# A state-space layer beside attention: chunked states and a scan replaced by a direct causal convolution

## The chip, the cores and the metric

The kernel runs on one core of a Trainium2 chip. A core has five engines, each with its own instruction stream in a fixed order: TensorE (PE) multiplies matrices, VectorE (DVE) and ScalarE (ACT) work on elements, GpSimd (POOL) and SyncE (SP) here mostly issue DMAs. The engines wait for one another by semaphores. The metric is the time of one execution on the device, in microseconds (us); the median of two executions before the change is 853.1 us (852.64 and 853.55).

## The reference

`x` has 2048 positions and 512 channels, all tensors are bf16. Two layers run on their inputs, and a gate mixes their outputs:

```python
g = sigmoid((x * gate_w).sum(-1, keepdims=True))
a = attention(x, wqkv, wo)          # 32 heads of 16, softmax over 2048 keys, not causal
dt = exp(log_dt)[:, None]           # B: 512 channels, 128 states each, complex
logdA = dt * (A_re + 1j * A_im);  dB = dt * (B_re + 1j * B_im);  C = C_re + 1j * C_im
P = exp(logdA[:, :, None] * arange(2048))
K = einsum("dn,dnl,dn->dl", C, P, dB).real      # 2048 taps for each channel
y = causal_convolution(u, K) + u * Dskip        # by an FFT in the reference
out = g * a + (1 - g) * y
```

The tap `K[d, l]` is a sum over 128 states of a coefficient times a complex root to the power `l`. The kernel reads `x` as the input of both layers.

## The kernel before, in words

**Attention.** The 2048 x 2048 scores of 32 heads are cut into 32 batches of four heads by 512 queries, and each batch into 64 tiles of 128 keys by 512 queries: 2048 tiles. Three tiles form a group (683 groups, counted by `g`). PE computes a group's scores with three products `SC<-Qm,KT` that stand side by side in rows of its array, into one of two PSUM buffers `SC0`, `SC1`; ACT takes their exp (`ex`, line 913: `ET<-SC`, 128x1536, or 128x1024 where one tile was given to DVE); PE multiplies with the values, four products `OA<-ET,VE` side by side in the columns of its array, a *quad*. Some tiles go to DVE instead, four of them in a *set*: `DZ<-SC` on line 949 makes an exponential by integer arithmetic on the bits of bf16, line 960 and the value products `OA<-DZ,..`, `OA<-DU,..` finish it. `WIN` says in which groups sets may be taken, `DVQ` how much spare time of DVE it needs, depending on which part of the other layer is done. After each batch DVE transposes and divides the sums (`norm_a`, `norm_b`, `norm_c`), and `early` multiplies the first three quarters of the queries with `Wo` during the attention, scales by the gate and stores them in DRAM (`od`).

**State-space layer.** Positions are cut into 32 chunks of 64. DVE makes the powers of the roots up to 64 (`table`, `PT<-tt,tt`), which go to DRAM (`ptd`) and come back transposed as `Qt`. Then for each of 16 blocks of 32 channels: `kstage` makes the 64 first taps (two quads `MB<-PT,wrb` and `MB<-PT,nwi`) and stores them (`kpd`); `sstage` makes each chunk's own state, 64 products `MB<-X,Qt` with 128 columns of weights and 32 moving columns, one for each chunk, at a step of 64 elements (`X2[qr](16 * bl + k, [[64, 32]], ...)`); DVE stores them as `SG`. `scan` runs over the chunks on DVE (lines 1333 to 1340: four operations of 512 columns for each of 30 chunks, twice) and POOL copies each result to `SG` by DMA. `ystage` then works on 32 half blocks: state times powers, `MB<-Py,SG`, in quads, and the part within a chunk with Toeplitz operands, `MB<-Tt,XY`. `Yst` is the result times the gate; it goes to DRAM (`ytd`), comes back transposed (`Yl`, `yread`), and `outs` adds it to the first three quarters of the output (`AR`, reloaded from `od`). The last quarter gets it in PSUM, from a product with the identity (`MB<-Yl,idb`) ahead of the output products (`ahead_of`).

**Order.** The program is laid out at build time. `Sched` holds one thread for each part of the other work, with a priority (a list near line 1651), and a planned cost for each operation. After each group's exp it fills the time until that exp's planned end with operations of the threads, in PE's and DVE's streams (`sch.fill(t, t + OVER, want)`). Operations left when the exps are all placed are put behind them. The PSUM bank `MB` belongs to one thread at a time (`LOCK`). Where PE would have too little to do, it gets filler products `OA<-wm` that add zero, by the columns that `FILL` and `REST` ask for.

**The end.** After the last exp: the last value products, `norm_a` to `norm_c` of batch 31, four output products with `Wo`, four copies `fo`, four stores. `Wo` is loaded on SP behind the first output store of `outs`.

## Time and profile before

| what | value |
|---|---|
| median of the runs | 853.1 us (852.64 to 853.55) |
| span of the profiled execution | 854.3 us |
| first exp starts / first output product with `Wo` after the exps | 13.1 us / 844.85 us |
| ACT busy | 97% |
| DVE busy | 90% |
| PE busy, its weight loads | 89%, 35% |
| POOL busy | 5% |
| bytes moved by DMA | 94.55 MB |
| mean granted clock of TensorE | 0.985 |

The page of the profile gives busy time per engine, then the span in 40 equal slices, then the chain of work that ended last, followed back from the end to what released each step. In a row of a group of instructions, `out<-in` are the program's names for the operands, `x434` is the count, and behind the first bar stand the busy time in us and the mean duration of one in ns; behind the second the engine's idle time just before them and what ended it. A timeline row gives start and duration in us. Instructions of one engine overlap in part, so the mean duration is longer than the distance from one start to the next. The profiled execution gives no time of its own beside its span.

### The profile page before, as it was taken

Reading aid. Unit: us, or ns where it says so; the run is one execution under the profiler, and the core shown is the slowest. Engines: PE = TensorE matmul, PEld = TensorE weight load, DVE = VectorE, ACT = ScalarE, POOL = GpSimd, SP = SyncE. Lnnn points to the kernel's source line nnn. Section 1 sums busy time; section 2 is a strip of 40 time slices with the busy share of each in tenths; the row PEclk is TensorE's granted clock in tenths of the full one; section 3 lists DMA queues with packets and bytes.
Section 4 is the critical chain, followed back from the end, with each engine's and each line's share of the span. In section 5 each row is a group of like instructions: output and inputs, shape, how many; then the busy total and the mean of one; then the engine's idle time right before and its main releaser. Section 6 shows DMA issues by size and latency. Waiting matters only on the chain.

```text
span 854.3 us, 23568 instructions
## 1 busy us (share of the span) xinstructions
PE 756.7 (89%) x10301; PEld 296.5 (35%) x10301; DVE 766.1 (90%) x1271; ACT 826.1 (97%) x695; POOL 44.0 (5%) x73
## 2 busy tenths in 40 slices
PE   7888888788768999999999899889988899999986
PEld 3232332222212434343443344334442234443321
DVE  5799999999969988898898999999999978997994
ACT  6999999999979999999999999999999999999996
POOL 4000000000000000000010111101111100000000
PEclk9999999999989999899998999999999999999999
DMA  9400102942933498477394597248998425645120
GB/s 206 118 2 10 35 3 82 194 153 81 73 129 152 51 206 103 149 131 164 62 162 71 84 192 116 36 104 166 199 191 151 120 88 121 136 120 113 25 99 26
DMA packets 218168, 94.55 MB, mean 111 GB/s; under 512 B 185168, under 2 KB 205008, under 8 KB 216016
## 3 DMA queue, kind: packets, MB, share of 16 engines
q1 hardware_dynamic: 207408, 83.99, 45.6%
q0 software_dynamic: 8640, 7.87, 5.9%
q8 instruction: 81, 1.33, 0.6%
q10 hardware_dynamic: 2016, 1.18, 0.6%
q14 instruction: 23, 0.19, 0.1%
HBM read 35.17 MB, written 30.82 MB: 77 GB/s over the span
## 4 chain that ended last, share of the span: by engine, by line
ACT 66%; PE 23%; DMA 5%; DVE 4%; SPq 1%; issue 0%; ACTq 0%; DVEq 0%
ACT ET L913 65%; PE OA L632 9%; PE SC L632 7%; PE MB L632 7%; DMA gm_gd<-g 3%; DMA gm_ytd<-Yst 1%; DMA gm_ptd<-PT 1%; DVE DZ L949 1%; DMA Wq<-in_A_wqkv_dram 1%; DVE s L1333 1%; DVE s L1335 1%; DVE G L1340 0%; DVE s L1338 0%; DVE tt L1007 0%; SPq L1488 0%
## 5 line engine op out<-in xcount | busy, mean ns | idle before, releaser
L913 ACT ACTIVATE ET<-SC 128x1536 bf16<-128x1536 f32 (+1 forms) x683 | 817.8, 1508 | 15.1 <-PE SC L632 13.9
L632 PE MATMUL SC<-Qm,KT 32*128 32x512 bf16 x2048 | 276.5, 387 | 75.9 <-ACT ET L913 61.1
L632 PE MATMUL OA<-wm 128*32 128x256 bf16 (+3 forms) x2193 | 251.6, 341 | 1.2 <-DVE wm L685 1.2
L632 PE MATMUL OA<-ET,VE 128*32 128x512 bf16 x1800 | 181.6, 395 | 4.6 <-DVE OT L984 4.4
L949 DVE TENSOR_SCALAR DZ<-SC 128x512 uint16<-128x512 f32 x248 | 166.2, 685 | 19.1 <-PE SC L632 16.8
L632 PEld LDWEIGHTS SC<-Qm,KT 32*128 32x128 bf16 x2048 | 70.7, 91 | 291.8 <-ACT ET L913 233.9
L632 PEld LDWEIGHTS OA<-wm 128*32 128x32 bf16 (+2 forms) x2193 | 72.9, 95 | 33.8 <-issue 15.5
L632 PEld LDWEIGHTS OA<-ET,VE 128*32 128x32 bf16 x1800 | 46.1, 93 | 106.1 <-issue 98.4
L632 PE MATMUL MB<-X,Qt 64*128 64x32 bf16 x1024 | 74.5, 231 | 0.0
L632 PEld LDWEIGHTS MB<-X,Qt 64*128 64x128 bf16 x1024 | 57.7, 109 | 25.2 <-issue 23.0
L1310 DVE TENSOR_SCALAR SG<-MB 128x512 bf16<-128x512 f32 x64 | 43.9, 686 | 10.6 <-PE MB L632 9.8
L960 DVE TENSOR_SCALAR DZ<-DZ 128x2048 uint16<-128x2048 uint16 x62 | 42.5, 685 | 8.2 <-PE OA L632 8.2
L1342 POOL DMA_DIRECT2D SG<-G x60 | 33.0, 550 | 255.7 <-DVE G L1340 250.9
L1340 DVE TENSOR_TENSOR G<-s,s 128x512 f32<-128x512 f32 x60 | 41.2, 687 | 3.1
L960 DVE TENSOR_SCALAR DU<-DZ 128x2048 uint16<-128x2048 uint16 x62 | 42.3, 685 | 0.4
L1333 DVE TENSOR_TENSOR s<-G,MU 128x512 f32<-128x512 f32 x60 | 41.2, 687 | 1.0
L1338 DVE TENSOR_TENSOR s<-s,SG 128x512 f32<-128x512 f32 x60 | 41.1, 685 | 0.0
L1335 DVE TENSOR_TENSOR s<-G,MU 128x512 f32<-128x512 f32 x60 | 41.0, 683 | 0.0
L1007 DVE TENSOR_TENSOR ft<-FP,L 128x1024 f32<-128x1024 f32 (+1 forms) x32 | 34.4, 1084 | 0.1
L1007 DVE TENSOR_TENSOR PT<-tt,tt 128x1024 bf16<-128x1024 bf16 x48 | 32.8, 683 | 0.4
L632 PEld LDWEIGHTS MB<-Py,SG 128*32 128x32 bf16 x1024 | 29.6, 165 | 8.2 <-issue 4.1
L984 DVE STREAM_TRANSPOSE OT<-OA 128x512 f32<-128x512 f32 x32 | 22.8, 712 | 9.2 <-PE OA L632 8.8
(166 smaller groups left out, 625.6 us busy)
## 6 DMA issues: line engine op xcount, KB each, us to landing
gm_ptd<-PT SPq DMA_DIRECT2D x16, 1024.0 KB, 6.1
Py<-gm_ptd SPq DMA_DIRECT2D x32, 512.0 KB, 5.0
SG<-G POOLq DMA_DIRECT2D x60, 128.0 KB, 3.1
gm_kpd<-Kst SPq DMA_DIRECT2D x16, 256.0 KB, 3.5
Tt<-gm_kpd SPq DMA_DIRECT2D x128, 32.0 KB, 3.5
gm_xrd<-in_A_x_dram SPq DMA_DIRECT2D x1, 2048.0 KB, 13.2
X<-gm_xrd SPq DMA_DIRECT2D x8, 256.0 KB, 5.0
Wo<-in_A_wo_dram SPq DMA_DIRECT2D x4, 512.0 KB, 4.4
```

The source lines that it names most:

```text
L632: op("PE", lambda t: t.matmul(out(), lhsT(), rhs(), start=start, stop=stop, skip_group_check=True, **kw), R, W, c=c, lat=.15, a=a, cfg=cfg)
L913: op("ACT", lambda a: a.activation(ET(512 * e, [[1, 512 * n]]), sc(0, [[1, 512 * n]]), AF.Exp, scale=DH ** -0.5), [(sc, i, g) for i in ran ...
L949: op("DVE", lambda v: v.tensor_scalar(z.u16(512 * k, [[1, 512 * n]]), sc(512 * na, [[1, 512 * n]]), XS, XB, ALU.mult, ALU.add), [(sc, na + ...
L960: op("DVE", lambda v: v.tensor_scalar(t.u16(0, [[1, 2048]]), z.u16(0, [[1, 2048]]), float(STEP[k][0]), None, ALU.add), R, W, c=.07 + 2048 ...
L984: op("DVE", lambda v: v.transpose(OT(512 * w, [[1, 512]]), OA(0, [[1, 512]])), [(OA, 0, b)], [(OT, w, b)], c=.64)
L1007: op(eng, lambda v: v.tensor_tensor(o(), a(), b_(), f), R, W, c=c)
L1310: op("DVE", lambda v, bank=bank, par=par, part=part: v.tensor_scalar(sg(2 * SGH + SGH * part + CB * k8 + 16 * par, [[2 * SGH, 32], [1, 16] ...
L1333: op("DVE", lambda v, g0=g0: v.tensor_tensor(s2(0, W), g0(0, W), MU(d0, [[0, 2], [1, 256]]), ALU.mult), [(g0, 0)] + key("MU"), [(s2, 0)], ...
L1335: op("DVE", lambda v, g0=g0: v.tensor_tensor(s3(0, W), g0(256, [[-256, 2], [1, 256]]), MU(D + d0, [[D, 2], [1, 256]]), ALU.mult), [(g0, 0) ...
L1338: op("DVE", lambda v, so=so: v.tensor_tensor(s2(0, W), s2(0, W), sg(so, W), ALU.add), [(s2, 0)] + ks, [(s2, 0)], c=F5)
L1340: op("DVE", lambda v, g1=g1: v.tensor_tensor(g1(0, [[1, 512]]), s2(0, [[1, 512]]), s3(0, [[1, 512]]), ALU.add), [(s2, 0), (s3, 0)], [(g1, ...
L1342: later("POOL", .3, 0, lambda so=so, g1=g1, c=c: dma("POOL", lambda e: e.dma_start(sg(so, [[1, 512]]), g1(0, [[1, 512]])), [(g1, 0)], [(sg ...
```

## The change

There are no states and no scan any more. The taps of all 2048 positions are made on PE from two tables of powers: `At` holds, for each channel and state, 32 powers with a step of 64 and the coefficient, `PT` 64 powers with a step of 1, left in two parts; `kstage` multiplies them over the states and adds the parts, products of 64 and of 48 columns. The skip weight enters as one more product (`sF`, `sE`). Taps go to DRAM (`kpd`) with 32 zeros ahead of each channel's. `kloads` reads them back 64 times, for 8 channels each, 1 MB at a time in four DMAs, as rows that overlap: partition `p` begins at tap `p + 1`, so that each 32 columns of `Kop` are a Toeplitz operand.

`x` lies in DRAM cut into chunks of 32 positions (`J`), 32 channels (`XB`) to an array; four copies of it, each 16 chunks later than the one before, fill the partitions of `X`. `ystage` is one unit for each block of 32 channels: a quad that clears the bank, then for each of 8 groups of four channels 16 quads `MB<-X,Kop`, quad `A` with 64 - `A` moving columns, one for each chunk, which lie 32 elements apart in `X`. The weights are 32 contiguous columns of `Kop`. There are 2048 such quads, 8192 products.

The result goes to `ytd` as before, and the chunks for the last quarter of the output also to `ybd`; both come back transposed, `Yl` and `Yb`. `outs` adds four arrays (positions ordered by their place in a chunk), two stores each. `early`'s result is stored for that order, `x` fills its last quarter in `od`, and the last four output tiles and `norm_c` follow the same order of positions. The tail's `norm_c` is one transpose in place of two halves.

The gate is computed early, behind the first value projections. `FILL` goes from 1600 to 1300 and `REST` away; `WIN` and `DVQ` have new numbers. By the order, 85 sets go to DVE (62 before), and ACT has 342 long and 341 short exps (434 and 249).

The diff, cut to its core:

```diff
-FILL = 1600
+FILL = 1300
-REST = (14, 1, 1792, 425)
-SGAT = (195, 260)
-SMM = .035
+J = 32
+NC = S // J
+KR = S + J
+KG = 8
+NK = 3
+YAT = 140
+XB = 32
-WIN = ((180, 400, 2, 1), (400, 640, 2, 1), (640, 678, 3, 2))
-DVQ = (("scan1", 0.2), ("scan0", 0.8), ("S15", 2.0), (None, 0.7))
+WIN = ((262, 330, 2, 1), (330, 678, 3, 2))
+DVQ = (("tabs", 0.2), (None, 0.7))
+KMM = .055
+YMM = .055
+YSEG = 2
...
     def kstage(blk):
-        for part, wn in ((0, "wrb"), (1, "nwi")):
-            yield ("PE", QUAD)
-            for a in range(4):
-                mm(lambda a=a: MB(0, [[1, 512]], 32 * a, 32), lambda wn=wn: B[wn](CB * blk, [[1, 32]]),
...
+        for i in range(8):
+            yield ("PE", 4 * KMM)
+            for x in range(2):
+                for k in range(2):
+                    n = T - 16 * k
+                    for j in range(4):
+                        mm(lambda i=i, j=j, n=n: MB(64 * i + T - n, [[1, n]], 32 * j, 32),
+                           lambda i=i, j=j, x=x: At(NA * (2 * (a0 + 4 * i + j) + x), [[1, NA]]),
+                           lambda i=i, j=j, x=x, k=k, n=n: PT(k * PA + n * (2 * (4 * i + j) + x), [[1, n]]),
...
+    def kloads():
+        for v in range(D // KG):
+            K, blk = B[f"Kop{v % NK}"], v * KG // CB
+            yield ("AFTER", f"g{YAT}")
+            yield ("AFTER", f"kd{blk}")
+            if v >= NK:
+                yield ("AFTER", f"yv{v - NK}")
+            for a in range(4):
+                yield ("SP", .6)
+                dma("SP", lambda e, a=a, v=v, K=K: e.dma_start(K(0, [[512, KG], [1, 512]], 32 * a, 32),
+                                                               kpd.dram(v * KG * KR + 1 + 512 * a, [[1, 32], [KR, KG], [1, 512]])),
...
     def ystage():
-        def unit(u):
...
+        for u in range(NBLK):
+            k, r2 = CB * u // XB, u % 2
...
+            for i in range(8):
+                v = (CB * u + 4 * i) // KG
...
+                for A0 in range(0, 16, YSEG):
+                    yield ("PE", YSEG * YMM)
+                    for A in range(A0, A0 + YSEG):
+                        for j in range(4):
+                            mm(lambda i=i, j=j, A=A: MB(64 * i + A, [[1, NC - A]], 32 * j, 32),
+                               lambda i=i, j=j, A=A, K=K: K(((4 * i) % KG + j) * 512 + 32 * A, [[1, 32]]),
+                               lambda i=i, j=j, A=A, X=X, u=u: X((CB * u + 4 * i + j) % XB, [[XB, NC - A]]),
...
     def outs():
...
+        for k in range(4):
+            AR = B[f"AR{k}"]
+            yield ("DVE", 1.2, 0)
...
         yield ("SP", .5)
         wo_load(B["Wo"])
...
-        mm(lambda: b(off, NAT), lambda: idb(0, [[1, P]]), lambda: Yl(lt * D, PERM), [(idb, 0)] + [(Yl, x) for x in range(NBLK)],
+        mm(lambda: b(off, [[1, D]]), lambda: idb(0, [[1, P]]), lambda: Yb(i * D, [[1, D]]), [(idb, 0)] + [(Yb, x) for x in range(NBLK)],
```

Three places show how rows move. The first is PE's stream near group 200. Before, a stretch of the states' products (`MB<-X,Qt`; `DZ`, `DU`, `VS` belong to DVE's sets):

```order
L632 MATMUL MB<-X_177,Qt 128x32 x16
L632 MATMUL OA<-ET,VE 32x512 x4
L632 MATMUL OA<-wm 32x512 x4
L632 MATMUL SC<-Qm,KT 128x512 x3
L632 MATMUL OA<-ET,VE 32x512 x4
```

Now:

```order
L619 MATMUL SC<-Qm,KT 128x512 x3
L619 MATMUL OA<-ET,VE 32x512 x4
L619 MATMUL MB<-X_193,Kop_190 32x58 x4
L619 MATMUL MB<-X_193,Kop_190 32x57 x4
L619 MATMUL MB<-X_193,Kop_190 32x56 x4
L619 MATMUL MB<-X_193,Kop_190 32x55 x4
L619 MATMUL MB<-X_193,Kop_190 32x54 x4
L619 MATMUL MB<-X_193,Kop_190 32x53 x4
L619 MATMUL MB<-X_193,Kop_190 32x52 x4
L619 MATMUL MB<-X_193,Kop_190 32x51 x4
L619 MATMUL MB<-X_193,Kop_190 32x50 x4
L619 MATMUL MB<-X_193,Kop_190 32x49 x4
```

Up to ten quads of the convolution stand between one group's values and the next group's scores, where a filler or sixteen products of the states stood.

The second is the end of PE's stream. Before, behind the last scores:

```order
L632 MATMUL SC<-Qm,KT 128x512 x2
L632 MATMUL OA<-wm 32x512 x12
L632 MATMUL OA<-ET,VE 32x512 x4
L632 MATMUL OA<-wm 32x512 x4
L632 MATMUL MB<-Yl,idb 128x512
L632 MATMUL MB<-Wo,OnT_74 128x512 x3
```

Now the last of the 280 quads that follow the last scores, and what comes behind them:

```order
L619 MATMUL MB<-X_193,Kop_189 32x52 x4
L619 MATMUL MB<-X_193,Kop_189 32x51 x4
L619 MATMUL MB<-X_193,Kop_189 32x50 x4
L619 MATMUL MB<-X_193,Kop_189 32x49 x4
L619 MATMUL MB<-Yb,idb 128x512
L619 MATMUL MB<-Wo,OnT_73 128x512 x3
L619 MATMUL SC<-Yb,idb 128x512
L619 MATMUL SC<-Wo,OnT_73 128x512 x3
L619 MATMUL OA<-ET,VE 32x512 x4
```

The last values of the attention now stand behind the products with `Wo` that need the last block of the convolution, and that block is computed behind the last scores.

The third is the end of SP's queue. Before:

```order
L1419 DMA gm_ytd<-Yst 128x4x64
L1432 DMA_TRANSPOSE Yl<-gm_ytd 128x16x32
L1546 DMA out_dram<-AR_76 128x4x512
L636 DMA Wo<-in_A_wo_dram 128x4x512
L1546 DMA out_dram<-AR_79 128x4x512
L1546 DMA out_dram<-AR_82 128x4x512
L1503 DMA out_dram<-fo 128x512 x2
```

Now, with the last loads of `Kop` ahead:

```order
L1236 DMA Kop_189<-gm_kpd 32x8x512 x4
L1294 DMA gm_ytd<-Yst 128x8x64
L1297 DMA gm_ybd<-Yst 128x8x16
L1304 DMA_TRANSPOSE Yl<-gm_ytd 128x16x32
L1307 DMA_TRANSPOSE Yb<-gm_ybd 128x4x32
L1401 DMA out_dram<-AR_68 48x4x512 x2
L1401 DMA out_dram<-AR_70 48x4x512 x2
L623 DMA Wo<-in_A_wo_dram 128x4x512
L1401 DMA out_dram<-AR_72 48x4x512 x2
L1401 DMA out_dram<-AR_74 48x4x512 x2
L1356 DMA out_dram<-fo 8x16x512 x2
```

The load of `Wo` stands behind four stores of the output, which wait for the last block's transpose.

More of the change, by code (lines that the diff above doesn't have):

```diff
@@ L32 @@
 DMARG = 1.2
-PTM = 2.4
 ZLAG = .6
@@ L1413, in unit @@
[L1413 to L1415 removed]
+                mm(lambda j=j: MB(0, [[1, 512]], 32 * j, 32), lambda: wm(0, [[1, 32]]), lambda: wm(0, [[1, 512]]), [(wm, 0)], ky, True, False,
+                   pos=(0, 32 * j), c=QUAD if j == 0 else 0, a=128, cfg="C")
```

749 lines of the change are left out of this document (289 added, 460 removed).

## The prediction, made before the result was known

> **What bounds the kernel now.** I read the busy shares first, then the chain of work that ended last.
>
> ```profile
> span 854.3 us, 23568 instructions
> PE 756.7 (89%) x10301; PEld 296.5 (35%) x10301; DVE 766.1 (90%) x1271; ACT 826.1 (97%) x695; POOL 44.0 (5%) x73
> PEclk9999999999989999899998999999999999999999
> ...
> ACT 66%; PE 23%; DMA 5%; DVE 4%; SPq 1%; issue 0%; ACTq 0%; DVEq 0%
> ```
>
> ACT is busy 97% of the span and owns two thirds of the chain, PE a quarter. The profiled execution took 854.3 us as a span, the only time it gives; the two runs have a median of 853.1, so the span reads 1.2 us long. What ACT does is exp, in two shapes:
>
> ```profile
> L913 ACT ACTIVATE ET<-SC 128x1536 bf16<-128x1536 f32 x434 | 593.6, 1713 | 9.7 <-PE SC L632 9.3
> L913 ACT ACTIVATE ET<-SC 128x1024 bf16<-128x1024 f32 x249 | 242.0, 1151 | 5.4 <-PE SC L632 4.7
> ```
>
> There are 683 exps, and what they wait for is PE's next scores. Their means overlap one another, so the time that one costs has to be read from stretches in which ACT does nothing else:
>
> ```profile
> 58.04 153.65 ACT L913 ACTIVATE ET<-SC 128x1536 bf16<-128x1536 f32 x114
> 210.98 0.81 ACT L1473 ACTIVATE ge<-gp 128x16 f32<-128x16 f32 x1
> ...
> 718.83 125.19 ACT ET L913 x121
> ...
> L913 ACT ACTIVATE ET<-SC 128x1024 bf16<-128x1024 f32 x88 | 83.7, 1210 | 0.0
> L913 ACT ACTIVATE ET<-SC 128x1536 bf16<-128x1536 f32 x33 | 47.4, 1612 | 0.1
> ```
>
> From 58.04 to 210.98 are 114 long exps: 152.94/114 = 1.342 us each. The chain's piece at 718.83 holds 121 exps, by the groups of that window 33 long and 88 short: (125.19 - 33 x 1.342)/88 = 0.919 us per short one. So all exps cost 434 x 1.342 + 249 x 0.919 = 811.2 us. The end:
>
> ```profile
> 843.60:854.30 10.70, 5.95 (x40) 1.91 (x32) 3.63 (x8) 2.50 (x4) 0.00 (x0) 0.90 0.16 51
> ...
> 844.06 0.40 PE L632 MATMUL OA<-ET,VE 128*32 128x512 bf16 x4 [0.19 <-ACT ET L913]
> 844.85 0.81 PE L632 MATMUL MB<-Wo,OnT 128*128 128x512 bf16 x3
> 846.91 0.72 DVE L984 STREAM_TRANSPOSE OT<-OA 128x512 f32<-128x512 f32 x1 [6.46 <-PE OA L632]
> 851.19 0.36 ACTq L1503 DMA_DIRECT2D out_dram<-fo  x1
> ```
>
> The last exp ends near 844.9. The first of the output products stands at 844.85, and from there to the end is 9.4 us. The first exp starts at 13.1 in the trace, so **854.3 = 13.1 head + 811.2 exps + 20.6 in which ACT does not run at that rate + 9.4 tail.** The 20.6 is PE being late:
>
> ```profile
> 228.60:283.20 54.60, 42.44 (x510) 12.91 (x502) 45.32 (x82) 49.90 (x41) 0.52 (x1) 0.94 0.37 114
> 331.00:380.00 49.00, 48.17 (x621) 20.22 (x618) 43.28 (x72) 46.40 (x42) 0.00 (x0) 0.93 0.69 130
> 677.10:843.60 166.50, 152.41 (x2365) 58.65 (x2364) 141.48 (x232) 166.38 (x164) 0.53 (x1) 1.00 0.37 91
> ```
>
> (Stretch, its length, busy time of PE, weight loads, DVE, ACT and POOL, clock, DMA share, GB/s.) In the first two, ACT is short of the stretch by 4.7 and 2.6 us, and the granted clock is 0.94 and 0.93; in the last ACT is never idle, and the clock 1.00.
>
> **The change part by part.** *Exp.* Before, 62 sets of four score tiles go to DVE, after it 85; 2048 - 340 = 1708 tiles stay on ACT, as 342 long and 341 short exps: 342 x 1.342 + 341 x 0.919 = 772.4 us, 38.8 less. That is what the change can win, as far as PE and DVE follow.
>
> *DVE.* It takes 23 more sets and loses the scan:
>
> ```profile
> L949 DVE TENSOR_SCALAR DZ<-SC 128x512 uint16<-128x512 f32 x248 | 166.2, 685 | 19.1 <-PE SC L632 16.8
> L1340 DVE TENSOR_TENSOR G<-s,s 128x512 f32<-128x512 f32 x60 | 41.2, 687 | 3.1
> ```
>
> 92 more tiles by 0.67 are 62 us; the scan's four operations of this kind and count give back 4 x 41.2 = 165. The new tables take most of the rest, early on. I take nothing, since DVE's work per stage stays under ACT's; by its share of 90% it could cost up to 10 us where the sets are dense.
>
> *PE, removed and added.* The states' 1024 products, their 1024 readers, 512 Toeplitz products and 1716 of the 1872 column-packed fillers `OA<-wm` go. In come 512 quads that make the taps, moved at unit step, and 2048 quads of four column-packed products `MB<-X,Kop`, with 64 down to 49 moving columns (56.5 on average) whose step is 32 elements. No row shows such a quad. What it takes, c, decides this case, and there are four rows near it:
>
> ```profile
> 287.52 0.40 PE L632 MATMUL OA<-ET,VE 128*32 128x512 bf16 x4
> 287.85 1.08 PE L632 MATMUL MB<-X,Qt 64*128 64x32 bf16 x16
> 288.86 0.29 PE L632 MATMUL OA<-wm 128*32 128x256 bf16 x4
> 289.09 0.39 PE L632 MATMUL SC<-Qm,KT 32*128 32x512 bf16 x3
> 289.41 0.40 PE L632 MATMUL OA<-ET,VE 128*32 128x512 bf16 x4
> 289.63 0.39 PE L632 MATMUL OA<-DZ,VS 128*32 128x512 bf16 x4
> 289.85 0.28 PE L632 MATMUL OA<-wm 128*32 128x256 bf16 x4
> ...
> 333.07 1.02 PE MB L632 x16
> 336.83 0.55 PE MB L632 x8
> ...
> 561.22 0.50 PE L632 MATMUL MB<-Py,SG 128*32 128x64 bf16 x16
> 561.54 0.28 PE L632 MATMUL OA<-wm 128*32 128x256 bf16 x4
> ```
>
> A packed quad of 512 contiguous columns takes 0.22 (289.41 to 289.63), 0.42 ns per column, and 0.32 (289.09 to 289.41) with a change of the array's shape, which is then 0.105. So four streams run side by side, and with contiguous columns c would be 56.5 x 0.42 = 0.024. But `MB<-X,Qt` moves 32 columns with a step of 64 elements: 16 take 1.02 and 8 take 0.55, so 8 more take 0.47, 59 ns each or 1.84 ns per column, over four times as long. At that rate, with four streams still side by side, c = 56.5 x 1.84 = **0.104**. One after another they would take 4 x 0.104 = 0.42, which the `Py,SG` row speaks against: its four packed weight loads per quad read 32 strided columns each, 128 in all, and a quad takes 0.32/4 = 0.080. If that were the rate at which strided columns can be read (0.62 ns each), c = 226 x 0.62 = 0.141. I take 0.10, the row nearest in kind, and keep 0.03 and 0.141 as ends.
>
> The page "SBUF — State Buffer" of the Trainium skill (the passage on SBUF cachelines, in Door 1) says that a read that goes to a new 16-byte line each time pays, and that eight bf16 are the free reach. The 59 ns agree with it, and by it 32 elements pay as 64 do; a size it does not give.
>
> The page "TensorE: Matmul & The Clock Gate" of the Trainium skill (Wait — 56ns, not 53.3ns?) has start to start never under about 25 ns, however few the columns, which would make c 0.10 without any stride, and leave the sum as it is. The `Py,SG` row, 16 in 0.32 us, has 20 ns, so the trace does not bear it out for packed products.
>
> *Where PE passes ACT.* By the order, 40 groups at 200 to 239 need 40 score triples and 30 value quads at 0.216, 79 turns at 0.105, and taps and bank starts, together 27.8 us, and 324 c: 60.2 at 0.10 against 40 x 1.342 = 53.7 for ACT, 6.5 over. At 240, 280 and 320 the same count gives 50.1 against 47.8, 48.5 against 46.1 and 41.5 against 41.4, so **11 us** in all; before 200 and after 360 ACT covers PE's sums, by little from 400 on. Taps at 0.055 to 0.10 a quad stand where PE needs 40 of 53.7 us: nothing. The point from which PE is late is c = 0.080 in the first of these stages. Unevenness I leave at 20.6, since PE and ACT stay as close as before. The last exp then ends at 13.1 + 772.4 + 20.6 + 11 = **817**.
>
> *Work behind the last scores.* Before, the last result of the state-space part, `Yst`, precedes the end by 51 us:
>
> ```profile
> 803.54 0.39 DVE L1414 TENSOR_TENSOR Yst<-MB,gt 128x256 bf16<-128x256 f32 x1
> ...
> 803.96 0.39 SPq L1419 DMA_DIRECT2D gm_ytd<-Yst  x1
> 805.82 1.23 SPq L1432 DMA_TRANSPOSE Yl<-gm_ytd  x1
> 815.26 0.51 SPq L636 DMA_DIRECT2D Wo<-in_A_wo_dram  x1
> ...
> X<-gm_xrd SPq DMA_DIRECT2D x8, 256.0 KB, 5.0
> Wo<-in_A_wo_dram SPq DMA_DIRECT2D x4, 512.0 KB, 4.4
> Yl<-gm_ytd SPq DMA_TRANSPOSE x16, 2.8
> ...
> L1007 DVE TENSOR_TENSOR PT<-tt,tt 128x1024 bf16<-128x1024 bf16 x48 | 32.8, 683 | 0.4
> ```
>
> After it, 1120 products, 280 quads, follow the last scores: 28 at 0.10, and 4 for three blocks' hand-overs of the bank. Each needs its operand: 8 loads of 1 MB, three buffers, four issues near 0.5 each. So at a small c SP bounds this at 2 to 3 us per load, 18 to 26 in all; with DMA at 0.37 of its time for 91 GB/s, 1 MB at full share is 4.3 us, 37 in all. I take 32: Y ends at 849.
>
> Then nothing covers the way out: 0.65 for `Yst`, 1.9 until the transpose is issued, 2.8 until it lands, two of the four adds (2048 bf16 columns each, twice the 0.68 of the row of 1024, 2.7 for both), 0.5 of issues, and only then is `Wo` loaded, since it stands behind the first outputs on SP: 4.4. From 803.96 to 815.26 the same way took 11.3 with DVE occupied, so up to 4 more. `Wo` is there 13 us after Y, and the output products, the last values, the norms and the stores take the 9.4: 23 in all, where 9.4 stood. **817 + 32 + 23 = 872**, 2% over the 853.1 if the span reads right and 1 less by the runs.
>
> *Nothing for* the removed state DMA of POOL (5% busy), the gate that comes early (its 21 us write holds SP while two score batches are loaded), and the 17 more loads at the start, behind the first exps' operands. If the gate's write held a batch's queries up, it would cost up to 21.
>
> **Rivals.** *Cheap quads.* If the step costs little, PE falls under ACT everywhere (at 0.055 the stage at 200 needs 45.6 of 53.7). Then 13.1 + 772.4 + 10 to 20 + 26 + 23 = 845 to 855, say **850**: not slower. For it: the step is half that of `X,Qt`, and column packing could hide the reads of one stream behind another. It decides from c under 0.08. *Reads that collide.* At c = 0.141 the overhang grows from 11 to 72 by the same sums and the tail by 11: **944**. For it: the `Py,SG` row; against: its weights are loaded, not moved. *The clock.* With the fillers gone, PE is at 40 of 53.7 us before group 160, less than the 42.4 of 54.6 in the stretch that had 0.94. The 0.94 over 54.6 us would be one stretch of 6.6 us at half clock (0.06 x 54.6 / 0.5); one such every 40 us, at 3 us each, 20 of them: **932**. For it are the three dips of the clock line; against, that they cost nothing where ACT has room. *It does not do what it says:* if DVE can't carry the 85 sets, ACT waits, and the forecast moves up by the 10 above.
>
> **How the numbers follow.** The forecast, 855 to 892 by c of 0.085 to 0.115, gets 0.46; cheap quads (834 to 855, the lower end with 8 of unevenness and 18 of loads) 0.28; colliding reads 0.14; the clock 0.08; the rest 0.04. The range goes from 835 to 935 and leaves out part of the two upper ones. Under 2% a measurement of this kernel can hardly be told from no change, so same means 836 to 870: 0.19 from cheap quads and 0.21 from the forecast; their 0.09 below 836 is the chance of faster.
>
> **What would show it.** The start-to-start time of `MB<-X,Kop` quads in an unbroken run gives c directly; ACT's waits for scores should sit between groups 200 and 330; the last exp near 817; then 25 to 35 us of PE alone, and 23 from the last Y product to the end, with `Wo` issued after an output store. I am wrong if c is under 0.08, or over 0.12, if exps wait for scores before group 160, or if the loads of `Kop`, not PE, set the pace.

## The result, and the profile after

The changed kernel takes 953.2 us (two runs, 953.17 and 953.27) against 853.1 before: a ratio of 1.116, with a 95% interval of 1.110 to 1.122. It is slower by 100 us, and lies above the range that was given (835 to 935).

The page of the changed kernel (busy time of each engine, clock in 40 slices, share of the chain that ended last, PE's instruction queue as packets, MB and share):

```profile
span 951.4 us, 35452 instructions
PE 809.7 (85%) x16143; PEld 379.6 (40%) x16170; DVE 727.3 (76%) x1316; ACT 797.9 (84%) x694; POOL 13.4 (1%) x13
PEclk7877999999999998999989999999999999999676
...
q8 instruction: 127, 2.08, 1.0%
...
PE 56%; ACT 28%; DMA 5%; DVE 4%; issue 4%; SPq 2%; ACTq 0%; DVEq 0%
```

ACT is busy 28 us less than before, as it should be with fewer exps, but over a span 97 us longer. The chain has turned round: PE owns 56% of it where ACT owned 66%. One line of the page plays no part in the prediction: the queue that brings PE its own instructions. Before it had

```profile
q8 instruction: 81, 1.33, 0.6%
```

Both are pieces of 16 KB, 256 records each: a product, its weight load and each wait of PE for a semaphore are a record each (20,704 records in 81 pieces before). The new kernel needs 127 of them.

Four stretches of the changed kernel (columns as in the prediction): the exps of groups 0 to 39, those of groups 200 to 239, from the last exp to the last product of Y, and the way out.

```profile
13.00:70.80 57.80, 50.61 (x476) 16.77 (x479) 41.44 (x79) 55.46 (x43) 1.38 (x1) 0.77 0.75 85
302.80:372.60 69.80, 63.04 (x1831) 41.67 (x1827) 38.01 (x76) 56.98 (x41) 0.00 (x0) 0.97 0.88 180
866.80:921.80 55.00, 29.86 (x1060) 27.10 (x1048) 1.38 (x2) 0.01 (x1) 0.00 (x0) 0.78 0.70 135
921.80:951.40 29.60, 7.20 (x23) 2.25 (x24) 10.50 (x12) 1.17 (x2) 0.00 (x0) 0.66 0.36 100
```

The last exp ends at 866.8, where 844.9 stood before and 817 was forecast. Y needs 55.0 us after it (forecast 32), the way out 29.6 (forecast 23). So the 951.4 is 13.0 + 853.8 + 55.0 + 29.6, and two of these four parts hold most of the miss: 50 us among the exps, 23 behind them.

What PE waited for in the changed kernel (us in total, times, longest):

```profile
PE SC L619 <- ACT ET L899: 47.8, 104, 1.0
PE MB L619 <- issue: 28.2, 32, 5.9
PE MB L619 <- DMA X<-gm_xrd: 17.3, 2, 13.1
PE MB L619 <- DMA Wo<-in_A_wo_dram: 14.7, 1, 14.7
...
PE MB L619 <- DMA Kop<-gm_kpd: 1.1, 1, 1.1
```

(L619 is the helper that records every product, L899 the exp.) The second line is a wait for nothing that the profile can name, up to 5.9 us long. PE's waits without a releaser before the change were at most 0.3 us. The loads of `Kop`, 64 MB in all, hold PE up by 1.1 us directly.

PE behind the last scores, and two rows of SP:

```profile
868.87 5.98 PE L619 MATMUL MB<-X,Kop 128*32 128x64 bf16 x219
877.38 2.67 PE L619 MATMUL MB<-X,Kop 128*32 128x64 bf16 x90 [1.07 <-DMA Kop<-gm_kpd]
885.90 3.56 PE L619 MATMUL MB<-X,Kop 128*32 128x58 bf16 x127 [5.86 <-issue]
905.22 9.04 PE L619 MATMUL MB<-X,Kop 128*32 128x64 bf16 x337 [13.15 <-DMA X<-gm_xrd]
916.98 4.70 PE L619 MATMUL MB<-X,Kop 128*32 128x60 bf16 x175 [2.71 <-issue]
936.35 1.46 PE L619 MATMUL MB<-Wo,OnT 128*128 128x512 bf16 x3 [14.67 <-DMA Wo<-in_A_wo_dram]
```

```profile
898.07 0.57 SPq L1253 DMA_DIRECT2D X<-gm_xrd  x1
...
931.03 0.71 SPq L623 DMA_DIRECT2D Wo<-in_A_wo_dram  x1
```

337 products, 84 quads, in 9.04 us are 0.107 each: the quad of four strided streams is what was forecast. The waits between the pieces are the news.

For the comparisons below, ACT's own pace is the time from start to start where exps follow each other without a gap, 1.330 us for a long one and 0.904 for a short one. What a range of groups takes beyond its exps at that pace is its *lateness*. "Piece stops" are the sum of PE's idle times ahead of every 256th record of the whole program, counted over products, weight loads and PE's waits for semaphores in the order of their starts.

| kernel | time | lateness, groups 0–79 | 80–159 | 160–359 | 360–679 | last exp | span after it | piece stops |
|---|---|---|---|---|---|---|---|---|
| before | 853.1 | 1.4 | 1.4 | 18.5 | 7.8 | 844.9 | 9.4 | 1.4 |
| after | 953.2 | 14.5 | 0.6 | 52.0 | 23.4 | 866.8 | 84.6 | 28.3 |
| e1_step1 | 949.2 | 15.2 | 0.8 | 57.2 | 14.3 | 864.9 | 82.5 | 71.4 |
| e1_step4 | 939.7 | 13.0 | 1.6 | 49.5 | 14.5 | 855.5 | 82.4 | 63.5 |
| e1_step8 | 953.6 | 13.8 | 0.9 | 50.6 | 24.4 | 866.3 | 85.5 | 27.6 |
| e2_small_kop | 911.3 | 13.6 | 0.9 | 29.9 | 16.8 | 836.5 | 73.0 | 3.5 |
| e3_both | 879.0 | 13.0 | 0.7 | 7.5 | 8.7 | 806.9 | 70.3 | 30.0 |
| e4_gate | 930.8 | 1.0 | 6.3 | 53.6 | 21.3 | 861.6 | 67.4 | 29.6 |
| e5_poolx | 944.1 | 13.4 | 0.7 | 56.2 | 22.9 | 867.9 | 74.4 | 38.9 |
| e6_contig | 944.0 | 12.9 | 11.2 | 61.1 | 58.1 | 928.6 | 13.6 | 93.1 |
| e10_tail | 920.6 | 1.0 | 5.3 | 52.1 | 22.7 | 859.2 | 59.5 | 27.7 |

(The trace of the changed kernel lacks 27 products, so its records are counted there by the weight loads, of which none is missing: 19.2 us of the stops lie ahead of the last scores, 9.2 behind them.)

### The profile page after: what moved, and what is told of

The parts are those of the page before. It is cut to its first block, busy times and chain, and to the rows that moved or that the text cites. A ratio compares the mean times of both kernels' runs of the same rounds, so it can differ in the third digit from the quotient of the medians.

```text
span 951.4 us, 35452 instructions
## 1 busy us (share of the span) xinstructions
PE 809.7 (85%) x16143; PEld 379.6 (40%) x16170; DVE 727.3 (76%) x1316; ACT 797.9 (84%) x694; POOL 13.4 (1%) x13
## 4 chain that ended last, share of the span: by engine, by line
PE 56%; ACT 28%; DMA 5%; DVE 4%; issue 4%; SPq 2%; ACTq 0%; DVEq 0%
ACT ET L899 28%; PE MB L619 25%; PE SC L619 16%; PE OA L619 15%; DMA gm_qd<-Qs 2%; DMA X<-gm_xrd 1%; SPq L1236 1%; DVE DZ L935 1%; DMA Wq<-in_A_wqkv_dram 1%; DVE OnT L989 1%; DMA Wo<-in_A_wo_dram 1%; DMA Kop<-gm_kpd 1%; DVE ON L982 0%; DMA Yl<-gm_ytd 0%; DVE DU L946 0%
## 5 line engine op out<-in xcount | busy, mean ns | idle before, releaser
L899 ACT ACTIVATE ET<-SC 128x1024 bf16<-128x1024 f32 (+1 forms) x683 | 789.9, 1337 | 65.2 <-PE SC L619 59.1
L619 PE MATMUL SC<-Qm,KT 32*128 32x512 bf16 x2048 | 281.4, 397 | 57.6 <-ACT ET L899 46.8
L619 PE MATMUL MB<-X,Kop 128*32 128x49 bf16 (+15 forms) x8192 | 269.7, 281 | 35.1 <-DMA X<-gm_xrd 17.3
L935 DVE TENSOR_SCALAR DZ<-SC 128x512 uint16<-128x512 f32 x340 | 227.2, 684 | 38.8 <-PE SC L619 35.3
L619 PEld LDWEIGHTS MB<-X,Kop 128*32 128x32 bf16 x8192 | 202.3, 111 | 91.2 <-issue 71.0
L619 PE MATMUL OA<-ET,VE 128*32 128x512 bf16 x1708 | 176.0, 405 | 2.8 <-issue 1.5
L619 PEld LDWEIGHTS SC<-Qm,KT 32*128 32x128 bf16 x2048 | 69.9, 91 | 256.9 <-ACT ET L899 166.8
L619 PE MATMUL OA<-wm 32*128 32x512 bf16 (+3 forms) x474 | 141.8, 410 | 2.3 <-DVE wm L671 1.2
L619 PEld LDWEIGHTS OA<-ET,VE 128*32 128x32 bf16 x1708 | 43.9, 94 | 101.3 <-issue 98.2
L946 DVE TENSOR_SCALAR DZ<-DZ 128x2048 uint16<-128x2048 uint16 x85 | 58.1, 684 | 7.3 <-PE OA L619 7.2
L970 DVE STREAM_TRANSPOSE OT<-OA 128x512 f32<-128x512 f32 x32 | 22.8, 711 | 19.5 <-PE OA L619 19.3
L619 PEld LDWEIGHTS OA<-wm 32*128 32x128 bf16 (+2 forms) x474 | 33.3, 94 | 9.2 <-issue 7.9
L619 PE MATMUL OA<-DZ,VS 128*32 128x512 bf16 x340 | 34.0, 389 | 0.9 <-DVE DZ L946 0.9
L619 PE MATMUL OA<-DU,VS 128*32 128x512 bf16 x340 | 33.7, 386 | 0.8 <-DVE DU L946 0.8
L619 PE MATMUL MB<-PT,At 128*32 128x64 bf16 (+1 forms) x2048 | 26.1, 192 | 9.0 <-issue 9.0
L619 PE MATMUL OA<-DZ,VE 128*32 128x512 bf16 x340 | 33.8, 388 | 0.0
L619 PEld LDWEIGHTS MB<-PT,At 128*32 128x32 bf16 x2048 | 23.6, 95 | 17.8 <-issue 13.6
L619 PE MATMUL MB<-Wo,OnT 128*128 128x512 bf16 x43 | 14.8, 413 | 16.7 <-DMA Wo<-in_A_wo_dram 14.7
L1217 DVE CAST Kst<-MB 128x512 bf16<-128x512 f32 x16 | 11.0, 686 | 22.9 <-PE MB L619 16.3
```

The lines of the kernel that those rows point to most:

```text
L619: op("PE", lambda t: t.matmul(out(), lhsT(), rhs(), start=start, stop=stop, skip_group_check=True, **kw), R, W, c=c, lat=.15, a=a, cfg=cfg)
L899: op("ACT", lambda a: a.activation(ET(512 * e, [[1, 512 * n]]), sc(0, [[1, 512 * n]]), AF.Exp, scale=DH ** -0.5), [(sc, i, g) for i in ran ...
L935: op("DVE", lambda v: v.tensor_scalar(z.u16(512 * k, [[1, 512 * n]]), sc(512 * na, [[1, 512 * n]]), XS, XBI, ALU.mult, ALU.add), [(sc, na ...
L946: op("DVE", lambda v: v.tensor_scalar(t.u16(0, [[1, 2048]]), z.u16(0, [[1, 2048]]), float(STEP[k][0]), None, ALU.add), R, W, c=.07 + 2048 ...
L970: op("DVE", lambda v: v.transpose(OT(512 * w, [[1, 512]]), OA(0, [[1, 512]])), [(OA, 0, b)], [(OT, w, b)], c=.64)
L1217: op("DVE", lambda v: v.tensor_copy(Kst(512 * (blk % 2), [[1, 512]]), MB(0, [[1, 512]])), ky, [(Kst, blk % 2, blk)], c=.66)
```

## The experiments

Kernels measured together ran on one chip beside a run of the kernel before: 853.9 for e1_step1, e1_step4, e1_step8 and e2; 852.6 for e3 to e6; 854.2 for e7 to e10. Each experiment is one execution.

### The reads or the loads

The first theory was that of the prediction: the strided reads of `X` make PE late, and everything after it. The rival was the 64 MB of `Kop` loads. Three kernels keep every product and move its columns at another step; one keeps the strided products and loads 64 of the 512 columns of each row from the fourth `Kop` on; the last does both.

```diff
-  X((CB * u + 4 * i + j) % XB, [[XB, NC - A]])
+  X((CB * u + 4 * i + j) % XB, [[1, NC - A]])     # e1_step1; 4 and 8 in the two others
```

> The changed kernel with one edit: the products MB<-X,Kop read X at a step of 1 element where they read at 32; the convolution is computed on wrong columns of X, all instructions and their order stay. Theory R (the step sets the 105 ns per quad in unbroken runs, and this makes PE late between groups 160 and 360): a quad takes 25 to 35 ns, as MB<-PT,At does at unit step (29), groups 200 to 239 take 54 to 58 us where they took 69.8, the last exp ends at 815 to 830 where it ended at 866.8, and the time is 885 to 905. Rival L (the 64 MB of Kop loads set the pace): groups 200 to 239 stay above 65 us and the time stays above 930.

> As the run at a step of 1, with a step of 4 elements (8 bytes, two columns to each 16 bytes); the convolution is computed on wrong columns. If what costs is that each column lies in a new 16-byte piece (the Trainium skill, SBUF - State Buffer, the passage on SBUF cachelines: two hits per line are enough for full rate), the quad takes 25 to 35 ns and the time is that of the step of 1. If any step beyond 1 costs, the quad takes 50 ns or more and the time lies 10 to 40 above that of the step of 1.

> As the run at a step of 1, with a step of 8 elements (16 bytes, a new 16-byte piece for each column); the convolution is computed on wrong columns. By the 16-byte reading the quad takes 100 to 108 ns, the same as at 32, and the time stays within 5 us of 953. If the price grows with the distance, it lies between that of the step of 4 and that of 32, at 60 to 95 ns, and the time at 905 to 940.

```diff
+  w = 512 if v < NK else 64
-  K(0, [[512, KG], [1, 512]], 32 * a, 32), kpd.dram(v * KG * KR + 1 + 512 * a, [[1, 32], [KR, KG], [1, 512]])
+  K(0, [[512, KG], [1, w]], 32 * a, 32), kpd.dram(v * KG * KR + 1 + 512 * a, [[1, 32], [KR, KG], [1, w]])
```

> The changed kernel with one edit: of the 64 loads of Kop all but the first three bring 64 of each 512 taps (an eighth of the bytes), so later products use stale taps; the same instructions, DMA issues and waits in the same order. Theory R: groups 200 to 239 keep 66 to 70 us, the last exp stays at 860 to 867, and only the tail gains, 5 to 12 us of Kop waits behind the last scores: 940 to 948. Rival L: groups 200 to 239 fall under 60 us, the last exp comes before 840, and the time falls under 920.

> Both earlier edits at once: the products MB<-X,Kop read X at a step of 1, and all but the first three loads of Kop bring an eighth of the bytes; the convolution is computed on wrong columns and stale taps, instructions and waits in the same order. Theory of two limits, each of which hides the other (the step's 105 ns per quad, and the loads of Kop): groups 160 to 359 lose nearly all of the 52 us over ACT's own time, the last exp ends at 815 to 828, the tail from there to the last Y product is 20 to 35, and the time is 865 to 885. If SP's order alone is the limit (the same issues in the same order, whatever they carry), the last exp stays above 835 and the time above 895.

A quad fell to 0.028 us at step 1; at step 4 it took 0.053, at step 8 0.100, at 32 it had taken 0.101. (These are medians from start to start.) The page "SBUF — State Buffer" of the Trainium skill, in the passage on cachelines in Door 1, says that two hits in each 16-byte line are enough for full bandwidth, so that eight bf16 are free; step 4 makes two hits in each line, and here it costs twice the time of step 1, so the measured row stands against the rule. That the price stops growing at 8 agrees with lines of 16 bytes.

But the time did not follow the quad: 949.2, 939.7 and 953.6 us at steps 1, 4 and 8. The stretch of groups 200 to 239 in e1_step1, e2_small_kop and e3_both:

```profile
301.10:376.60 75.50, 47.68 (x1794) 25.33 (x1791) 38.52 (x78) 55.50 (x42) 0.00 (x0) 0.80 0.82 165
```

```profile
298.20:362.30 64.10, 61.19 (x1831) 41.44 (x1827) 38.05 (x76) 56.53 (x41) 0.00 (x0) 1.00 0.32 46
```

```profile
293.60:349.30 55.70, 41.55 (x1815) 23.12 (x1802) 38.43 (x78) 54.39 (x41) 0.00 (x0) 0.97 0.37 53
```

With cheap quads PE is busy for only 47.7 us, and the stretch takes 75.5, more than the 69.8 of the changed kernel. With few bytes and dear quads it takes 64.1, between what the two theories gave for it, and PE is busy for nearly all of it: that is the limit of the prediction. Only with both does ACT set the pace, 55.7, and the last exp ends at 806.9, a little earlier than expected. From there to the last product of Y it is 40.3 us, longer than the 20 to 35 expected: the last `X` still comes late (10.9 us), and stops without a releaser take 14.0. So there are two limits, one behind the other: the first theory alone falls, and its rival alone does too.

What stops PE in e1_step1 while it has only 47.7 us of work shows in its rows (a stretch without gaps is left out where dots stand):

```profile
305.18 0.48 PE L619 MATMUL MB<-X,Kop 128*32 128x60 bf16 x23 [1.50 <-issue]
...
309.13 0.20 PE L619 MATMUL MB<-X,Kop 128*32 128x50 bf16 x3
313.02 0.84 PE L619 MATMUL MB<-X,Kop 128*32 128x50 bf16 x37 [3.69 <-issue]
...
317.23 0.40 PE L619 MATMUL MB<-X,Kop 128*32 128x53 bf16 x17 [0.68 <-issue]
```

The stops come in the middle of a run of equal products, in which nothing is waited for. They stand ahead of the records 7617, 7873 and 8129 of PE's stream, 256 apart, and 31 more stops of that kernel are whole multiples of 256 away from them, to within a record. A packet of 16,384 bytes of the instruction queue lands at 311.6 us, 1.4 us before PE goes on at 313.02. The changed kernel shows the same: behind 100 us it has 22 waits of over 0.25 us without a releaser; 20 of them stand at every 256th record (to within two), and PE goes on between 1.2 and 1.7 us after the landing of such a packet each time. PE has used up its instructions and waits for the next piece. Where both ends of a piece are such stops, the distance between them is the time in which a piece is supplied: 6.5 us as the median of 15 in e1_step1, and 4.2 of 14 in e3_both, whose DMAs are loaded less (0.37 of their time for 0.82). Behind the last scores of e3_both:

```profile
812.87 1.53 PE L619 MATMUL MB<-X,Kop 128*32 128x58 bf16 x127 [2.70 <-issue]
817.19 1.77 PE L619 MATMUL MB<-X,Kop 128*32 128x58 bf16 x127 [2.80 <-issue]
821.54 0.64 PE L619 MATMUL MB<-X,Kop 128*32 128x58 bf16 x39 [2.57 <-issue]
```

127 products, their 127 weight loads and two waits for semaphores are the 256 records of a piece; they are 1.5 to 1.8 us of work, and come every 4.3 us. The stretch of groups 200 to 239 holds 3658 records, 14.3 pieces; at ACT's 53.2 us that leaves 3.7 us for a piece. Piece stops add up to 71.4 us in e1_step1 and 3.5 in e2_small_kop. The dearer the quad, the fewer they are: 71.4, 63.5 and 27.6 us at steps 1, 4 and 8.

### The gate, and who issues the loads

The first 80 groups of the changed kernel are 14.5 us late, before any quad. SP of the changed kernel shows why:

```profile
58.58 2.65 SPq L1333 DMA_DIRECT2D gm_gd<-g  x4
61.27 0.62 SPq L1335 DMA_DIRECT2D gm_gd<-g  x1
61.93 4.59 SPq L1432 DMA_DIRECT2D gm_qd<-Qs  x1
76.26 1.73 SPq L727 DMA_DIRECT2D Qm<-gm_qd  x4
```

The gate's writes go ahead of a batch's queries, whose own write lands 14.3 us after its issue, and the scores of that batch wait for it. Experiment e4 computes the gate where it was before, after all projections.

```diff
-        yield ("AFTER", "V0.3")
+        yield ("AFTER", "projs")
```

> The changed kernel with the gate put back behind all projections, as before the change; nothing is left out. Theory: the gate's two writes, issued at 59.9, keep the write of the queries of batch 2 in the queues for 14.3 us, and this makes the exps of groups 40 to 79 late by 9.9 us; with the gate later they are late by under 3 and the last exp ends 8 to 14 earlier than 866.8, with 940 to 946 in all. Rival: the half clock of these groups, 40 to 85 us, is what makes them late; then 6 us or more of the 9.9 stay, and the time is 948 to 955.

The lateness of groups 0 to 79 goes from 14.5 to 1.0. The groups 0 to 39 of e4 and the next 40:

```profile
13.00:68.00 55.00, 43.50 (x431) 16.26 (x432) 44.54 (x84) 53.79 (x42) 0.00 (x0) 0.99 0.67 92
68.00:121.60 53.60, 42.09 (x558) 15.40 (x562) 51.36 (x107) 53.60 (x41) 0.00 (x0) 1.00 0.05 11
```

Both suspects go with this edit, the write and the half clock; e3_both tells them apart. Its gate stands early, its clock is full from 11.6 to 69.6 us, and its groups 40 to 49, which wait for those queries, are 11.5 us late all the same (9.1 in the changed kernel); its groups 20 to 39 are on time, where the changed kernel loses 3.2 in them at half clock. So the write costs most of it, and the half clock some 3 us.

The last exp comes only 5.2 us earlier. Groups 150 to 159 are now 5.4 us late, at half clock and with a piece stop of 2.8; the first exp starts 1.2 later, and in this order ACT has four more long exps (1.7 us). The kernel is faster than expected, 930.8, since the tail is 17 shorter: in this order of the streams the last `X` is loaded in time.

The next theory was that SP's queue, where loads of `Kop`, transposes and stores stand in line, is what delays things. Experiment e5 issues `Kop` and `X` on POOL, which has nothing else to do.

```diff
-                yield ("SP", .6)
-                dma("SP", lambda e, a=a, v=v, K=K: e.dma_start(K(...
+                yield ("POOL", .6)
+                dma("POOL", lambda e, a=a, v=v, K=K: e.dma_start(K(...
```

> The changed kernel with the loads of Kop and X issued by POOL where SP issued them; nothing is left out. Theory Q (the loads are late since SP issues in order and stands in waits for queries, taps and Yst ahead of them): groups 200 to 239 take 60 to 66 us, as with the small loads (64.1), the 13 us wait for X in the tail goes, and the time is 900 to 922. Theory B (the 64 MB are more than the DMA engines bring in that time): groups 200 to 239 stay at 68 or more, and the time at 935 or more.

The stretch of groups 200 to 239 takes 70.2 us (69.8 after), the last exp ends at 867.9. The queue is not what holds the exps up; that theory falls. The tail gains 10 us: the 13.1 us wait for `X` is gone and 24 quads now stand ahead of the last scores, but the piece stops behind them grow from 9.2 to 14.8.

### Contiguous operands

If the stride cost PE its time, one copy per block by DVE would take it away and leave the result right. Experiment e6 adds to e5 a copy of `X` with channel and chunk exchanged, and plans with 0.045 for a quad (0.035 for the taps). `X` itself has one buffer there, and the output's transposes begin only behind group 420.

```diff
+  op("DVE", lambda v, Xc=Xc: v.tensor_copy(Xc(0, [[NC, XB], [1, NC]]), X(0, [[1, XB], [XB, NC]])), ...
-  X((CB * u + 4 * i + j) % XB, [[XB, NC - A]])
+  X(((CB * u + 4 * i + j) % XB) * NC, [[1, NC - A]])
```

> A version that computes all of it: loads of Kop and X issued by POOL, and X copied once per 32 channels by DVE so that the 64 chunks of a channel are contiguous, which the products then read at a step of 1; planned with 45 ns per quad and 8 us per load, by which all products stand ahead of the last scores; ACT has 780.8 us of exps by the rows of before. With two limits gone: quads at 26 to 32 ns, last exp at 815 to 840, last Y product before it, way out 10 to 15, 830 to 855. If the bytes of Kop bound it all the same, the last exp is later than 855 and the time above 870.

The quads take 0.028, all of Y stands ahead of the last scores, and the way out is 13.6 us. The stretch from the last exp to the end, and PE's waits over the whole kernel:

```profile
928.60:942.20 13.60, 4.70 (x23) 1.60 (x21) 5.17 (x7) 1.19 (x3) 0.00 (x0) 0.81 0.12 39
```

```profile
PE MB L620 <- issue: 65.8, 34, 4.0
PE SC L620 <- ACT ET L900: 61.7, 145, 1.4
PE OA L620 <- issue: 16.8, 10, 4.5
```

Yet the last exp ends at 928.6, and the time is 944.0, 9 us better than the change and far from what was expected. The waits without a releaser now reach into the other work of PE (the value products `OA`); piece stops are 93.1 us in all. Cheaper quads use up 256 records sooner, and the supply does not follow.

### Is it the number of instructions, the bytes, or both

Three kernels test the piece theory away from the new layer, in the kernel before. Experiment e7 cuts each filler quad into four of a quarter of the columns, which brings PE's records from 20,704 to 32,944, about as many as the change has. Experiment e8 adds 64 copies of 1 MB from `x` to a scratch in DRAM, with the access pattern of the `Kop` loads. Experiment e9 does both.

```diff
-            for j in range(4):
-                zero(z, n, (0, 32 * j), 128, 32, ...
+            for h in range(4):
+                for j in range(4):
+                    zero(z, n // 4, (0, 32 * j), 128, 32, ..., n // 4 * h)
```

> The kernel before, with each filler quad of OA<-wm cut into four quads of a quarter of the columns: the same columns moved, no other work, in the same order, but PE has about 31,900 records in place of 20,704, near the 32,570 of the changed kernel. Theory I (PE's instructions come in pieces of 256 over the same DMA engines as the data, and PE stands when it uses a piece up before the next has landed, for which it takes both many instructions in a short time and busy DMA engines): stalls at every 256th record add 2 to 10 us, 855 to 864. Rival (the number of instructions alone costs): 880 or more.

```diff
+    def dummy():
+        for v in range(64):
+            yield ("AFTER", f"g{147 + 6 * v}")
+            for a in range(4):
+                dma("POOL", ... K.dram(((v % 4) * P + 32 * a) * 4096, [[4096, 32], [512, 8], [1, 512]]),
+                                dap(x_t, (v % 32) * 16640 + 1 + 512 * a, [[1, 32], [2080, 8], [1, 512]]) ...
```

> The kernel before, with 64 further copies of 1 MB each, in four DMAs of 256 pieces of 1 KB as the Kop loads are, one every six groups from group 147 on, issued by POOL from x to a part of DRAM that nothing reads. Theory I: with its 20,704 records PE is seldom caught, stalls at every 256th record add under 8 us, 853 to 866. Rival (the bytes themselves make queries, powers and states late): 875 or more, with exps waiting for scores whose PE waits name a data load.

> The kernel before with both: fillers cut in four and the 64 copies of 1 MB. Theory I: more than the sum of the two alone, stalls at every 256th record of 12 to 40 us in all, 868 to 900. Without that theory the two costs add, and no residue of 256 stands out in PE's stalls.

| kernel | time | over before | piece stops |
|---|---|---|---|
| e7_count | 872.3 | 18.2 | 6.5 |
| e8_bytes | 1014.8 | 160.7 | 2.6 |
| e9_both | 1036.4 | 182.2 | 80.9 |

The time of e7 is above what was expected of it, those of e8 and e9 far above. For the stops the answer is plain: neither the records (6.5) nor the bytes (2.6, one stop) make them, and both together make 80.9, more than expected. PE's waits of e8 and of e9:

```profile
PE MB L632 <- DMA Qt<-gm_ptd: 41.7, 8, 12.2
PE MB L632 <- issue: 19.5, 1, 19.5
```

```profile
PE OA L632 <- issue: 50.8, 24, 8.2
PE MB L632 <- issue: 21.1, 8, 7.1
PE SC L632 <- issue: 18.4, 9, 7.7
```

For the time the experiment says less. The copies are a heavier load than `Kop` (8.5 us from issue to landing at the median, against 5.4), and in e8 PE is late by data: 41.7 us for `Qt`. They were also not spread as meant: what says "after group 147" sets only the order in which a stream is written, POOL had nothing ahead of them, and 32 of the 256 DMAs were issued between 10.9 and 61 us, among the loads of the start; there 33 us are lost. In e9 the stops stand where e8 waited for data (between 345 and 440 us PE's long waits are 44 us in e8 and 40 in e9), which may be why the two costs only add up (18.2 + 160.7 = 178.9 for 182.2). The 19.5 us of e8's second line are no piece stop; what they are is not known.

Of e7's 18.2 the piece stops are 6.5. Its page shows two dips of the clock, and its rows a stop ahead of the first:

```profile
PEclk9999999999799999999999979999998999999999
```

```profile
227.84 0.58 PE L632 MATMUL SC<-Qm,KT 32*128 32x512 bf16 x1 [3.78 <-issue]
...
510.77 0.40 PE L632 MATMUL OA<-wm 128*32 128x64 bf16 x14 [1.45 <-issue]
```

The clock is at half from 226.9 to 240.5 and from 510.2 to 523.8, each time from within the stop that the row shows, the second of them a piece stop. What the first waits for, and how much of the remaining 11 us the half clock makes, stays open.

### A better tail

Experiment e10 takes e4, loads `Wo` ahead of the last transposes in place of behind the first output stores, and gives the loads of `X` an earlier turn.

```diff
+        yield ("AFTER", "yu13")
+        yield ("SP", .5)
+        wo_load(B["Wo"])
...
-                   (xloads(), 4), (early(), 1.5), (reload(), 5), (outs(), 6)):
+                   (xloads(), 3.5), (early(), 1.5), (reload(), 5), (outs(), 6)):
```

> The changed kernel with the gate behind all projections (930.8 us alone in an earlier run) and Wo loaded ahead of the last blocks' transposes; nothing is left out. The wait for Wo (7.7 us) goes, and what is late next is the output stores and Yb: 921 to 927.

It takes 920.6 us, at the lower end of what was expected: 33 less than the change, still 66 more than before. Behind its last scores nothing waits for `X` or `Wo` any more; the output products wait 6.8 us for the transposes of the last block, as was expected, and PE waits for pieces:

```profile
863.38 3.57 PE L619 MATMUL MB<-X,Kop 128*32 128x60 bf16 x127 [0.74 <-issue]
869.97 3.56 PE L619 MATMUL MB<-X,Kop 128*32 128x60 bf16 x127 [3.02 <-issue]
874.92 1.46 PE L619 MATMUL MB<-X,Kop 128*32 128x61 bf16 x49 [1.40 <-issue]
```

No version that was run beats the kernel before.

## Why the prediction was wrong

It forecast 872 and the time is 953, some 80 more: 50 among the exps, 23 in the work behind them and 7 on the way out. The rivals with the reads at 0.141 (944) and with half clock (932) come near it, but by mechanisms that are not what happened. By the steps of the prediction:

**The exps, 772.4: right in size.** In e3_both, where neither limit is left, the last exp ends at 806.9; the prediction's sum without its overhang, 13.1 + 772.4 + 20.6, is 806.1. That the two meet so closely is luck: 13.0 us of e3_both are the gate's, which the sum leaves out, and its groups 160 to 359 are 11 less late than before (7.5 for 18.5).

**The quad, 0.10: right.** It takes 0.101 to 0.107 us. The choice of the `X,Qt` row, by stride, was the right one of the four.

**PE's overhang of 11 us in groups 200 to 359: right as far as it goes.** The 18.5 of lateness that groups 160 to 359 had before and 11 make 29.5; e2_small_kop, where the bytes are gone, has 29.9. What failed is the sentence that after group 360 "ACT covers PE's sums, by little": in e2_small_kop it cost 9 us there (16.8 for 7.8), and with contiguous reads as well, in e3_both, 1 (8.7).

**The gate, priced at nothing: wrong.** The prediction gave it up to 21 if its write held a batch's queries up. It did, and it cost 13 (14.5 against 1.4 before in groups 0 to 79; e4 takes it away). Some 9 of these are in groups 40 to 49, which wait for the queries, and 3 in groups 20 to 39, at half clock. The condition was named, and the wrong end of it taken.

**The loads, priced at nothing ahead of the last scores: wrong, and the largest term.** "If the loads of `Kop`, not PE, set the pace" stood among what would make the prediction wrong, but the path thought of was a late `Kop`, and that cost 1.1 us. From e2_small_kop to the changed kernel the last exp moves by 30 us (836.5 to 866.8). Of these the trace shows 17.5 as piece stops (19.2 against 1.7) and 4 as a first wait for `X`; the other 9 have no single line, and half clock after the stops (0.97 of full in groups 200 to 239, 1.00 in e2) is part of them. That the loads act on PE's instruction supply is shown by the records 256 apart, and by e7 to e9; how the 30 divide is an estimate. 817 + 13 + 9 + 30 is 869, for 866.8 measured.

**Work behind the last scores, 32: wrong by 23.** The products take 28.2 us, as forecast. The waits between them are 25 in place of 4: 13.2 for `X`, which SP issues at 898 behind loads of `Kop` and transposes although its buffer was free 30 us earlier (with small loads, in e2_small_kop, this wait is still 10.6), 9.2 in piece stops, 1.1 for `Kop`, 1.6 for the hand-overs. The prediction took SP as a bound of 2 to 3 us a load, and left out that SP works in order.

**The way out, 23: 7 short.** `Wo` holds its products until 936.4, 14.5 after Y (13 forecast). The rest takes 15.1, for which the 9.4 of before was copied; but the products run at half clock until 941.3, behind a stretch in which PE stood still, with the last values now behind seven of them: 1.7 more until `norm_a`. `norm_c` takes 2.3 us where its two halves took 0.8 together, 1.5 more: it writes to columns 16 apart, and the 12 such transposes with contiguous columns take 0.70 each. The copies and stores take 2 more.

**The rivals.** Cheap quads, as e1_step1 has them, were to give 850; they gave 949, because the faster PE uses up its instructions sooner. Half clock at 932 had PE's low load before group 160 as its cause; half clock does stand there, and costs some 3 us. That the change does not do what it says is out: DVE carries its 85 sets at 76% busy.

The step that failed first is the model of PE's time itself: the sums counted columns per product, nothing for a record, and nothing for the loads that compete with PE's own instructions. In its place the runs showed that groups 200 to 239 need a piece every 3.7 us at ACT's pace, that pieces came 7.0 us apart where the changed kernel stopped for two in a row (median of 9), 28.3 us of such stops, and a last exp 30 us later with the full loads than with small ones. The other terms that failed are the gate's write at nothing (13) and the order of SP's queue in the tail (13.2 for `X`). The queue of instructions stood on the page of before with 81 packets, and the change's 12,000 more records could have been set beside it.

## What to carry to other kernels

Where a change turns a few wide products into many narrow ones, count PE's records, divide by 256, and set the time that each piece leaves beside the 4.2 us at which pieces came here when DMA was lightly loaded and the 6 to 8 when it was not; waits "for issue" in the middle of a run of equal products are the sign. When taking one suspected cost away leaves the time as it was, take both away before either is acquitted. A DMA moved ahead on an in-order queue is paid by what stands behind it, and an operand that is needed last must not be issued last.

## What the runs showed of the hardware

**PE's instructions are a DMA load of their own.** They come in packets of 16 KB for 256 records, PE stands still when one is late and goes on 1.2 to 1.7 us after it has landed (all 20 stops of the changed kernel), and other DMAs make it late. The distance between two such stops was 4.2 us (median of 14, e3_both), 5.8 (18, e1_step4), 6.5 (15, e1_step1), 6.3 (23, e6_contig) and 7.8 (10, e9_both, up to 15.5). In e7_count a piece was needed only every 6.3 us (4032 records from 340 to 440 us), and with the DMAs of the kernel before there were hardly any stops; with the copies beside it, in e9_both, there were 80.9 us of them. The page "Runtime: NRT & Kernel Launch" of the Trainium skill (Instruction fetch mechanics) says that instructions are refilled in blocks of 16 KB, 256 instructions, and that the cost of a block is mostly hidden. The size agrees; the cost was hidden in the kernel before (1.4 us in 81 pieces) and not in e6_contig (93.1 in 128).

**A strided moving operand costs by the step up to 8 elements:** 0.028, 0.053, 0.100 and 0.101 us for a quad at steps of 1, 4, 8 and 32 bf16. At the large step the clock makes no difference: less the 0.28 that the last one takes, the 127 products from 885.90, all at half clock, make 0.106 a quad, and the 337 from 905.22, of which all but the first 2 us run at full clock, 0.104. Four streams of such reads go on side by side, as was assumed.

**A write that stands behind small ones lands late:** 14.3 us for the queries' write behind the gate's.

**A transpose on DVE whose output columns lie 16 apart** takes 2.3 to 2.5 us (4 in the changed kernel), with contiguous columns 0.70 (12).

**The clock can drop within a stop of PE,** and stays at half for 13.6 us in e7_count around stops of 3.8 and 1.5 us. Stops are not its only companion: the kernel before has three stretches of 6.8 us at half clock without a stop over 0.5 us ahead of them. A stretch of 20 to 24 us at half clock lies over the gate's 64 products of one column in the changed kernel (from 40 us), e2_small_kop (38), e4_gate (218) and e10_tail (220); in e3_both and in the kernel before the same 64 run at full clock. Why was not tried.
